# Cosformer attention and routed experts on one core: attention written out by hand as one pipeline, keys weighted in place of values, expert weights loaded later

## The chip, the core and the metric

The kernel runs on one core of one Trainium2 chip. A core has TensorE (PE; its weight loads are shown as PEld), VectorE (DVE), ScalarE (ACT), GpSimd (POOL) and SyncE (SP). Each works through its own queue of instructions in order; they wait for each other through semaphores. Sixteen DMA engines move data for all of them; here SP and POOL issue transfers. The metric is the device time of one execution in microseconds (us).

## What is computed

```python
def phi(x, c, s):
    r = np.maximum(x, 0.0)
    return np.concatenate([r * c, r * s], axis=-1)
q_p, k_p = phi(q, cos_w, sin_w), phi(k, cos_w, sin_w)      # 8 batches, 8 heads, 576 x 64
kv = np.einsum('bhsf,bhsd->bhfd', k_p, v)
z = np.sum(k_p, axis=2)
attn = einsum(q_p, kv) / (einsum(q_p, z) + 1e-06)
x = attn.transpose(0, 2, 1, 3).reshape(4608, 512)
...
e_idx = np.argmax(x @ w_gate, axis=1)                       # one of 8 experts for a row
gate_w, eom = probability of that expert, sigmoid(x @ w_output_gate)
ye = np.maximum(x[mask] @ w1[e], 0.0) @ w2[e]               # 512 -> 1024 -> 512
out[mask] = gate_w * eom * ye
```

`cos_w` and `sin_w` depend on the position in the sequence alone.

## The kernel before

**Attention.** A batch has 576 positions: four chunks of 128 (position 4p + c on partition p) and a tail of 64; the tails of two batches share a chunk. `stage_k` (L227 to 256) makes the product of keys and values of a batch. For each half of the heads ScalarE takes the relu of k (L235), VectorE multiplies each chunk of v by the cosine and by the sine into `vcs`, 64 + 1 columns each, the 1 being the weight itself for the sum `z` (L243, L245), and TensorE multiplies four heads, two at a time in the two column halves of its array, 64 weight columns (k) by 130 moving ones, into `kvp` (L252). In float32 one matmul leaves two records in the trace. `stage_g` (L257 to 282) copies `kvp` into `kvm`, transposes a copy of it (`kvtp`) and multiplies by the gate weights (`kvgp`, L276), so that `kvm` has 16 columns of logits more.

A unit is one chunk of queries of one batch, 36 in all (4 in an even batch, 5 in an odd one). `stage_q` (L284 to 335) sorts the heads (L292), transposes (L300), takes the relu on the way out (`qT`, L302), multiplies 16 records of 64 by 162 into `qo` (L311), joins the cosine and sine halves (`t` on ScalarE L322, `u` on VectorE L323), divides on GpSimd into a row `xr` of 512 float16 values (L333) and sums the logits into `glog` (L331). `u`, `t` and `qo` have two buffers each.

**Routing.** After each two batches `route` (L337 to 395) finds each row's expert, ranks it with small matmuls (L374, L376), and GpSimd scatters nine chunks of rows into the list `xs` in DRAM by indirect DMAs (L391). Then some 24 small instructions on VectorE (L429 to L468) turn the counts into 43 slots: the first row of each (`rows_i`) and its expert (`evs`).

**Experts.** For each slot SP loads 128 rows of `xs` (`fetch`, L488), TensorE transposes them (`xtsp`, L502), VectorE copies them (`xts`, L517), eight matmuls make `hp` (L522), ScalarE takes the relu (`hs`, L526). The transposes of `hs` (`htsp`, L511), their copy (`hts`, L514), eight matmuls into `yp` (L533), the scaling (`ysb`, L537) and the scatter to the output (L539) come one turn later. TensorE reads the slot's expert from `evs` into a register (L498) and addresses the weights with it.

**Order and transfers.** A scheduler orders the first part; in the last one the orders of PE and SP are as written. `load_w(e)` (L170 to 172) brings both matrices of an expert from float32 to float16 through POOL's queue, 1 MB each in SBUF. They have a place of their own, so nothing holds them back, and the calls of the first experts are issued at the start. k, v and q come through SP in halves of 512 KB. A scatter waits for the one before it, since both write `xs`.

## Time and profile before

| what | us |
|---|---|
| median of 2 runs (575.81 to 576.67) | 576.24 |
| profiled execution | 572.66 |
| its span | 570.9 |
| TensorE busy, share of the span | 352.1 (62%) |
| VectorE busy | 255.9 (45%) |
| ScalarE, GpSimd busy | 138.1, 140.6 |
| mean granted clock | 0.845 |

A row of the profile gives a line of the kernel, an engine, an operation with the tile that it writes and those that it reads, how often it ran, and times. "Idle before" is the time in which the engine had nothing running just ahead, with what ended that. The granted clock is TensorE's, as a share of 2.4 GHz. A busy TensorE is not TensorE at its peak.

### The profile page before, as it was taken

What the parts mean: (1) busy time and instruction counts of PE and PEld (TensorE: products, weight loads), DVE (VectorE), ACT (ScalarE), POOL (GpSimd) and SP (SyncE); (2) the same over time, 40 slices, a digit from 0 to 9 for tenths busy, and PEclk for the clock granted to TensorE, in tenths of its full rate; (3) what the DMA queues carried; (4) which work ended last, traced back from release to release, by engine and by line L of the source; (5) the groups of instructions that cost most, each with busy time, mean ns of one, the idle gap of its engine ahead of it and who ended that gap; (6) DMA issues with size and microseconds to landing.
All of it is one profiled execution on the core that took longest, in us unless ns stands there. A gap on an engine that the chain in (4) does not pass through costs nothing. (4 is left out here: it accounts for less than half of the span.)

```text
span 570.9 us, 8672 instructions
## 1 busy us (share of the span) xinstructions
PE 352.1 (62%) x2764; PEld 231.0 (40%) x2764; DVE 255.9 (45%) x851; ACT 138.1 (24%) x239; POOL 140.6 (25%) x189
## 2 busy tenths in 40 slices
PE   0020368443677578576683004888898888888883
PEld 0020257332555366455572002444444444444441
DVE  7011248424476578668665501333333333333331
ACT  0000025122152425253442000222222222222220
POOL 6100004112025232533345320211122222222221
PEclk9985659776597959789966555999999999999998
DMA  7999988999083708450310012112222222222200
GB/s 135 240 206 229 242 216 225 235 242 230 25 229 105 222 11 229 121 178 18 102 47 28 28 37 65 63 67 82 84 75 84 79 84 74 68 84 77 73 36 2
DMA packets 65755, 66.79 MB, mean 117 GB/s; under 512 B 18734, under 2 KB 58158, under 8 KB 65712
## 3 DMA queue, kind: packets, MB, share of 16 engines
q0 software_dynamic: 17712, 30.98, 23.0%
q1 hardware_dynamic: 48000, 35.26, 22.8%
q8 instruction: 25, 0.41, 0.3%
q14 instruction: 18, 0.15, 0.1%
HBM read 67.61 MB, written 17.22 MB: 149 GB/s over the span
## 5 line engine op out<-in xcount | busy, mean ns | idle before, releaser
L522 PE MATMUL hp<-w1t,xts 128*128 x344 | 83.2, 385 | 25.1 <-DVE xts L517 25.1
L526 ACT ACTIVATE hs<-hp 128x512 f16<-128x512 f32 x86 | 51.4, 597 | 191.5 <-PE hp L522 191.5
L252 PE MATMUL kvp<-vcs,k 128*64 128x130 f32 x512 | 48.7, 347 | 63.6 <-DVE vcs L245 57.5
L539 POOL DMA_INDIRECT out_dram<-ysb,sidx x43 | 42.1, 980 | 177.2 <-DVE ysb L537 163.7
L533 PE MATMUL yp<-w2t,hts 128*128 x344 | 81.3, 379 | 1.1 <-DVE hts L514 1.1
L311 PE MATMUL qo<-kvm,qT 64*128 64x162 f32 x512 | 56.0, 359 | 41.9 <-DVE u L323 32.1
L333 POOL TENSOR_TENSOR xr<-u,rc 128x512 f16<-128x512 f32 x36 | 39.6, 1104 | 128.0 <-DVE rc L327 127.5
L537 DVE TENSOR_SCALAR ysb<-yp,xg 128x512 f32<-128x512 f32 x43 | 32.3, 751 | 82.8 <-PE yp L533 82.8
L252 PEld LDWEIGHTS kvp<-vcs,k 128*64 128x64 f32 x512 | 39.6, 177 | 71.0 <-issue 57.1
L323 DVE SCALAR_TENSOR_TENSOR u<-qo,sinc,t 128x324 f32<-128x324 f32 x72 | 38.9, 551 | 64.0 <-ACT t L322 36.4
L311 PEld LDWEIGHTS qo<-kvm,qT 64*128 64x128 f32 x512 | 45.1, 221 | 51.2 <-DVE u L323 36.4
L391 POOL DMA_INDIRECT xs<-xr,di x36 | 37.7, 1047 | 89.9 <-DMA xs<-xr,di 63.3
L522 PEld LDWEIGHTS <-xts 128*128 128x128 f16 x344 | 33.7, 98 | 60.5 <-DVE xts L517 28.6
L322 ACT ACTIVATE t<-qo,cosc 128x324 f32<-128x324 f32 x72 | 37.7, 529 | 57.0 <-PE qo L311 42.2
L533 PEld LDWEIGHTS <-hts 128*128 128x128 f16 x344 | 33.6, 98 | 41.6 <-DVE hts L514 1.2
L243 DVE TENSOR_SCALAR vcs<-v,cosc 128x256 f32<-128x256 f32 x64 | 23.3, 365 | 46.1 <-DMA v<-in_v_dram 44.2
L504 DVE COPY_PREDICATED_SCALAR sidx<-valid,xg 128x1 int32 x43 | 9.3, 217 | 74.3 <-DMA xg<-xs 74.3
L502 PE MATMUL xtsp<-ident,xg 128*128 128x128 f16 x172 | 17.1, 224 | 34.1 <-DMA xg<-xs 34.1
L235 ACT ACTIVATE k<-k 128x1024 f32<-128x1024 f32 x16 | 16.9, 1056 | 87.4 <-DMA k<-in_k_dram 87.4
L502 PEld LDWEIGHTS <-xg 128*128 128x128 f16 x172 | 13.4, 100 | 44.4 <-DMA xg<-xs 34.1
L514 DVE COPY hts<-htsp 128x1024 f16<-128x1024 f16 x43 | 29.3, 681 | 0.4 <-PE htsp L511 0.4
L302 ACT ACTIVATE qT<-qtp 128x512 f32<-128x512 f32 x36 | 20.0, 595 | 34.6 <-PE qtp L300 34.6
(132 smaller groups left out, 363.3 us busy)
## 6 DMA issues: line engine op xcount, KB each, us to landing
w1t<-in_moe_w_dram POOLq DMA_DIRECT2D x8, 1024.0 KB, 28.4
w2t<-in_moe_w_dram POOLq DMA_DIRECT2D x8, 1024.0 KB, 28.7
k<-in_k_dram SPq DMA_DIRECT2D x16, 512.0 KB, 13.9
v<-in_v_dram SPq DMA_DIRECT2D x16, 512.0 KB, 9.9
q<-in_q_dram SPq DMA_DIRECT2D x16, 512.0 KB, 5.5
xg<-xs SPq DMA_DIRECT2D x43, 129.0 KB, 2.1
xs<-zt SPq DMA_DIRECT2D x9, 129.0 KB, 9.9
kt<-in_k_dram SPq DMA_DIRECT2D x8, 128.0 KB, 6.8
```

The costliest lines, as they stand in the source:

```text
L252: PE.matmul(kvp[64 * ab:64 * ab + 64, hf, 130 * pr:130 * pr + 130], lhs, w[p0:p1, h, :], start=(c == 0 and pr == 0), stop=(c == 4), skip_g ...
L311: PE.matmul(qo[:, 2 * ab + pr, 0:162], qT[r0:r0 + 64, qd, :], kvms[b][r0:r0 + 64, 2 * qd:2 * qd + 2, :], start=True, stop=True)
L322: ACT.activation(t[:], qo[:, :, 0:81], AF.Copy, scale=cosc[:, c:c + 1])
L323: DVE.scalar_tensor_tensor(u[:, 4 * hf:4 * hf + 4, :], qo[:, :, 81:162], sinc[:, c:c + 1], t[:], ALU.mult, ALU.add)
L333: GP.tensor_tensor(xrow[:, 0:DM].bitcast(F16).rearrange("p (h d) -> p h d", d=D), u[:, :, 0:64], rc[:].unsqueeze(2).to_broadcast([P, H, D] ...
L391: GP.indirect_dma_start(out=xs[:, :], out_offset=bass.IndirectOffsetOnAxis(ap=di[:, c:c + 1], axis=0), in_=xr[:], in_offset=None)
L502: PE.transpose(xts_ps[:, kc, :], xg[:, kc * 128:(kc + 1) * 128].bitcast(F16), ident16[:, :])
L522: PE.matmul(hp[:], xts[:, kc, :], w1t[:, kc, bass.ds(ev, 1), fh * 512:(fh + 1) * 512], start=(kc == 0), stop=(kc == 3))
L526: ACT.activation(hs[:, fh * 512:(fh + 1) * 512], hp[:], AF.Relu)
L533: PE.matmul(yp[:], hts[:, fc, :], w2t[:, fc, bass.ds(evp, 1), :], start=(fc == 0), stop=(fc == 7))
L537: DVE.tensor_scalar(ysb[:], yp[:], xgp[:, DM + 2:DM + 4].bitcast(F32), None, ALU.mult)
L539: GP.indirect_dma_start(out=out[:, :], out_offset=bass.IndirectOffsetOnAxis(ap=sidx[:, jj:jj + 1], axis=0), in_=ysb[:], in_offset=None, bo ...
```

## The change

**Keys weighted.** `k_prep` makes relu(k) times cosine on ScalarE and max(k times sine, 0) on VectorE into `kc`, 512 columns each, for a chunk of all eight heads. `k_mm` multiplies 16 times for a chunk, 64 weight columns (weighted k) by 65 moving ones: v as it came, with a column of ones behind it. For that column v is loaded into rows of 65 values, by head, in pieces of 256 bytes. `vcs` and its 40 small copies are gone. ScalarE takes the relu of q while it sorts the heads (`q_prep`); the copy after the transposes is a plain one.

**One order for all engines.** From the first load on the order of every engine is as written. A unit issues `q_mm`, the transposes of the next unit (`q_tr`), the planned chunks of the next batch's keys, its own output (`q_out`), the relu of the unit after next, and a piece of the route of the two batches before. The evacuation of the keys' product goes to VectorE and ScalarE by halves. Rows `xr` have 14 buffers in place of 10. Scatters to `xs`, and those to the output, are declared to touch distinct rows, so that one does not wait for another.

**Weights.** k, v and q are loaded into the place of the weights of experts 4 to 7, a batch ahead. Experts 0 to 3 are loaded at units 14, 19, 24 and 31, 4 and 5 after the last scatter, 6 and 7 after slots 2 and 4. Each load raises `wsem` by 32; a slot waits until it has 32 for each expert up to its own (`wns`), through a second register load.

**Experts.** The rows of slot j + 1 are transposed and copied before layer 1 of slot j; layer 2 of slot j - 1 follows it. Rows are fetched four slots ahead. `xtsp` has one buffer and `yp` two, where it was the other way.

Cut to its core:

```diff
-    vcs = []
-    for c in range(5):
-        t = constp.tile([P, 4, 130], F32, name=f"vcs{c}")
-        for h in range(4):
-            DVE.tensor_copy(t[:, h, 64:65], cosc[:, c:c + 1])
-            DVE.tensor_copy(t[:, h, 129:130], sinc[:, c:c + 1])
-        vcs.append(t)
...
+    EW = 4 * F + 8 * DM
+    wt = wpool.tile([P, E, EW], F16, name="wt")
+    w1v = wt[:, :, 0:4 * F].rearrange("p e (c f) -> p e c f", c=4)
+    w2v = wt[:, :, 4 * F:EW].rearrange("p e (c d) -> p e c d", c=8)
+    wsem = tc.alloc_semaphore("wsem")
...
+        for d in (GP.dma_start(w1v[:, e], moe_w1[e].rearrange("(c p) f -> p c f", p=128)),
+                  GP.dma_start(w2v[:, e],
+                               moe_w2[e].rearrange("(c p) d2 -> p c d2", p=128))):
+            d.then_inc(wsem, 16)
+            tc.add_to_no_dep_group("w", d.ins)
...
+    kbuf = [own(7, 4096 * i).rearrange("p (h c d) -> p h c d", h=H, d=D) for i in range(2)]
+    qbuf = [own(6, 4096 * i).rearrange("p (h c d) -> p h c d", h=H, d=D) for i in range(2)]
+    KW = H * NC4 * 65 * 2
+    v0 = wt[:, 4:6, :].rearrange("p e w -> p (e w)")
+    vbuf = [v0[:, KW * i:KW * i + KW].bitcast(F32).rearrange(
+        "p (h c d) -> p h c d", h=H, d=65) for i in range(2)]
+    for i in range(2):
+        GP.memset(vbuf[i][:, :, :, 64:65], 1.0)
+    vtl = constp.tile([P, H, 65], F32, name="vtl")
...
-        for e in range(E + 1):
-            SP.dma_start(xs[e * REG:e * REG + P, :], zt[:])
...
+        def load_v(b):
+            for h in range(H):
+                SP.dma_start(vbuf[b % 2][:, h, :, 0:D],
+                             v[b, h, 0:512, :].rearrange("(p c) d -> p c d", c=NC4))
...
+        def k_prep(b, c):
+            if c == 4 and b % 2 == 1:
+                return
+            nm = "kc" if c < 4 else "ktc"
+            kc = wk.tile([P, 2, H, D], F32, name=f"{nm}{b}_{c}", tag=nm,
+                         bufs=2 if c < 4 else 1)
+            src = kbuf[b % 2][:, :, c, :] if c < 4 else tails[b // 2, "k"][:]
+            ACT.activation(kc[:, 0], src, AF.Relu, scale=cosc[:, c:c + 1])
+            DVE.tensor_scalar(kc[:, 1], src, sinc[:, c:c + 1], 0.0, ALU.mult, ALU.max)
...
+            kc = kcs.pop((b, c)) if c < 4 else ktcs[b // 2]
+            p0, p1 = (0, P) if c < 4 else (lo, lo + 64)
             for hf in range(2):
-                kt, vt = kts[b, hf], vts[b, hf]
-                ACT.activation(kt[:], kt[:], AF.Relu)
-                ktl, vtl = tails[g, "k"], tails[g, "v"]
-                if par == 0 and hf == 0:
-                    ACT.activation(ktl[:], ktl[:], AF.Relu)
-                for c in range(5):
-                    w = vcs[c]
-                    p0, p1 = (0, P) if c < 4 else (lo, lo + 64)
-                    src = vt[:, :, c, :] if c < 4 else vtl[p0:p1, 4 * hf:4 * hf + 4, :]
-                    DVE.tensor_scalar(w[p0:p1, :, 0:64], src, cosc[p0:p1, c:c + 1],
-                                      None, ALU.mult)
-                    DVE.tensor_scalar(w[p0:p1, :, 65:129], src, sinc[p0:p1, c:c + 1],
-                                      None, ALU.mult)
-                    for pr in range(2):
+                for pr in range(2):
+                    for cs in range(2):
                         for ab in range(2):
-                            h = pr + 2 * ab
-                            lhs = (kt[:, h, c, :] if c < 4
-                                   else ktl[p0:p1, 4 * hf + h, :])
-                            PE.matmul(kvp[64 * ab:64 * ab + 64, hf,
-                                          130 * pr:130 * pr + 130],
-                                      lhs, w[p0:p1, h, :],
-                                      start=(c == 0 and pr == 0), stop=(c == 4),
-                                      skip_group_check=True)
-        def stage_g(b):
+                            h = 4 * hf + pr + 2 * ab
+                            rhs = (vbuf[b % 2][:, h, c, :] if c < 4
+                                   else vtl[p0:p1, h, :])
+                            o = 130 * pr + 65 * cs
+                            PE.matmul(kvp[64 * ab:64 * ab + 64, hf, o:o + 65],
+                                      kc[p0:p1, cs, h, :], rhs,
+                                      start=(c == 0 and pr == 0 and cs == 0),
+                                      stop=(c == 4), skip_group_check=True)
...
+            DVE.tensor_copy(kvm[:, 0:4, 0:65],
+                            kvp[:, 0, 0:260].rearrange("p (a w) -> p a w", w=65))
+            ACT.copy(kvm[:, 4:8, 0:65],
+                     kvp[:, 1, 0:260].rearrange("p (a w) -> p a w", w=65))
+            kvc = wk.tile([P, 8, 64], F32, name=f"kvc{b}", tag="kvc", bufs=1)
+            DVE.tensor_copy(kvc[:], kvm[:, :, 0:64])
...
+            qr = wk.tile([P, 2, 4, D], F32, name=f"qr{b}_{c}", tag="qr")
+            ACT.activation(qr[:], src.rearrange("p (a r) d -> p r a d", r=2), AF.Relu)
...
+                d = GP.indirect_dma_start(
+                tc.declare_no_dep(d.ins, group="sc", reason="distinct rows")
+                tc.add_to_no_dep_group("sc", d.ins)
+                if c % 3 == 2:
+                    yield
...
+        load_k(0)
+        load_v(0)
+        load_tails(0)
+        load_k(1)
+        load_v(1)
+        for e in range(E + 1):
+            SP.dma_start(xs[e * REG:e * REG + P, :], zt[:])
+        load_q(0)
...
+        plan_even = [[0, 1], [2, 3], [4]]
+        plan_odd = [[0], [1, 2], [3, 4]]
...
+        wload = {14: 0, 19: 1, 24: 2, 31: 3}
...
+            if c == 0:
+                if b + 1 < B:
+                    load_q(b + 1)
+                if b % 2 == 0:
+                    load_qtail(g)
+                if b + 2 < B:
+                    load_k(b + 2)
+                    load_v(b + 2)
+                if b % 2 == 1 and g + 1 < NG:
+                    load_tails(g + 1)
...
+            q_mm(b, c)
+            nxt = units[i + 1] if i + 1 < len(units) else None
+            if nxt is not None:
+                q_tr(*nxt)
...
+                        nc_ = rest[rest.index(cc) + 1:]
+                        if nc_:
+                            k_prep(b + 1, nc_[0])
+                        k_mm(b + 1, cc)
+                if c == len(plan) - 1:
+                    gst["kvc"] = g_evac(b + 1)
+                    gst["kvT"] = g_tr(b + 1, gst["kvc"])
+                elif c == len(plan):
+                    g_mm(b + 1, gst["kvT"])
+                    if b + 2 < B:
+                        k_prep(b + 2, 0)
+            xr = wk.tile([P, XW], U16, name=f"xr{b}_{c}", tag="xr", bufs=14)
+            xrows.append(xr)
+            q_out(b, c, glog, xr, len(xrows) - 1)
...
+            if i in wload:
+                load_w(wload[i])
...
+        load_w(4)
+        load_w(5)
...
+        DVE.tensor_scalar(wns[:], ej[:], 32.0, 32.0, ALU.mult, ALU.add)
...
+        def layer1(j):
+            ev = PE.value_load(evs[0:1, j:j + 1], min_val=0, max_val=7)
+            wv = PE.value_load(wns[0:1, j:j + 1], min_val=32, max_val=256)
+            PE.wait_ge(wsem, wv)
...
+        late = {2: 6, 4: 7}
...
+            if j + 4 < NSLOT:
+                fetch(j + 4)
+            if j + 1 < NSLOT:
+                x_tr(j + 1)
+            if j >= 1:
+                hts = h_tr(j - 1)
             if j < NSLOT:
+                layer1(j)
             if j >= 1:
+                layer2(j - 1, hts)
+            if j in late:
+                load_w(late[j])
         ctx2.close()
```

The order on TensorE in the first units of batch 0. `kvp` is the product of batch 1's keys, `qtp` the transposes of a unit, `qo` its products; x4 and x16 count like instructions. Before:

```order
L311 MATMUL qo_0_0_449<-kvm_340,qT_0_446 128x162
L252 MATMUL kvp_371<-vcs_142,k_0_359 64x130 x4
L252 MATMUL kvp_371<-vcs_151,k_0_359 64x130 x4
L252 MATMUL kvp_371<-vcs_160,kt_262 64x130 x4
L252 MATMUL kvp_371<-vcs_124,k_1_363 64x130 x4
L252 MATMUL kvp_371<-vcs_133,k_1_363 64x130 x4
L252 MATMUL kvp_371<-vcs_142,k_1_363 64x130 x4
L252 MATMUL kvp_371<-vcs_151,k_1_363 64x130 x4
L252 MATMUL kvp_371<-vcs_160,kt_262 64x130 x4
L311 MATMUL qo_0_0_449<-kvm_340,qT_0_446 128x162 x3
```

And now, from the first unit of batch 0 to the third:

```order
L340 MATMUL qo_0_0_389<-kvm_336,qT_0_357 128x162 x4
L340 MATMUL qo_0_1_397<-kvm_336,qT_0_357 128x162 x4
L322 MATMUL qtp_1_405<-ident,qr_1_350 128x128 x4
L272 MATMUL kvp_415<-wt,kc_0_369 64x65 x16
L272 MATMUL kvp_415<-wt,kc_1_412 64x65 x16
L340 MATMUL qo_1_0_462<-kvm_336,qT_1_410 128x162 x4
L340 MATMUL qo_1_1_470<-kvm_336,qT_1_410 128x162 x4
L322 MATMUL qtp_2_478<-ident,qr_2_459 128x128 x4
L272 MATMUL kvp_415<-wt,kc_2_432 64x65 x16
L272 MATMUL kvp_415<-wt,kc_3_485 64x65 x16
```

All chunks of the next batch stood inside the first unit; now they are shared out behind the units, 16 half as wide matmuls in place of 8 for a chunk.

The last scatters to `xs` on POOL, with what each waits for (DMASW3 is one of eight semaphores that POOL's transfers use in turn). Before:

```order
L390 COPY xr_4_2511<-meta_2582 128x2
L391 DMA xs<-xr_0_2210,di_2601 36992x516 [waits DMASW2_49,DVE_49,Pool_49]
L391 DMA xs<-xr_1_2245,di_2601 36992x516 [waits DMASW3_49,Pool_49]
L391 DMA xs<-xr_2_2280,di_2601 36992x516 [waits DMASW4_49,Pool_49]
L391 DMA xs<-xr_3_2315,di_2601 36992x516 [waits DMASW5_49,Pool_49]
```

And now, with the loads of experts 4 and 5 (L166 and L167) behind the last one:

```order
L427 COPY xr_0_2311<-meta_2768 128x2 [waits DVE_49]
L428 DMA xs<-xr_0_2311,di_2766 36992x516 [waits Pool_49]
L427 COPY xr_1_2391<-meta_2768 128x2
L428 DMA xs<-xr_1_2391,di_2766 36992x516 [waits DMASW4_49,Pool_49]
...
L427 COPY xr_4_2719<-meta_2768 128x2
L428 DMA xs<-xr_4_2719,di_2766 36992x516 [waits DMASW3_49,Pool_49]
L694 ISA [waits DMASW4_49]
L166 DMA wt<-in_moe_w_dram 128x4x1024 [waits DMAHW3_49,DMAHW4_49,DMAHW2_49,DMAHW5_49,DMAHW1_49,DMAHW6_49,DMAHW0_49,DMAHW7_49,DMASW4_49,PE_49]
```

Before, each waits for the semaphore of the one just ahead; now for that of eight transfers ahead, and the small copies stand between.

TensorE's queue in a slot of the experts, where the register load stands. Before, at the end of layer 2 of the slot ahead, and then the start of layer 1:

```order
L533 MATMUL yp_4048<-w2t,hts_4031 128x512
L498 TENSOR_LOAD evs
L498 ISA x2
L502 LDWEIGHTS xg_3939 [waits DMAHW2_49]
...
L511 MATMUL htsp_4088<-ident_69,hs_4035 128x128
L522 LDWEIGHTS xts_4099 [waits DVE_49]
```

And now:

```order
L607 LDWEIGHTS hs_3002 [waits Activation_49]
...
L607 MATMUL htsp_3048<-ident_69,hs_3002 128x128
L613 TENSOR_LOAD evs
L613 ISA x2
L614 TENSOR_LOAD wns
L614 ISA x2
L623 LDWEIGHTS xts_2969 [waits wsem]
```

One load stood behind layer 2 and ahead of the transposes of the rows; two stand now between the transposes of `hs` and layer 1, which waits for `wsem` and no longer for a copy on VectorE.

## Rows read from the trace of the kernel before

**Rows 1.** Timeline of SP's issues: start, us, queue, line, count.

```profile
3.57 5.66 SPq L193 DMA_DIRECT2D xs<-zt  x9
...
158.90 0.61 SPq L214 DMA_DIRECT2D vt<-in_v_dram  x1
```

**Rows 2.** Windows: stretch, us, busy PE, PEld, DVE, ACT, POOL, clock, DMA, GB/s.

```profile
180.00:313.00 133.00, 88.67 (x874) 68.95 (x871) 91.34 (x306) 48.36 (x88) 53.20 (x66) 0.84 0.37 109
313.00:350.50 37.50, 1.17 (x15) 0.91 (x15) 9.85 (x45) 0.47 (x2) 10.33 (x19) 0.50 0.12 39
350.50:562.60 212.10, 186.50 (x1200) 99.81 (x1199) 80.41 (x169) 51.36 (x86) 41.15 (x42) 0.99 0.21 71
```

**Rows 3.** Windows of line 331 alone, the sum of a unit's logits on VectorE.

```profile
180.00:313.00 133.00, 8.72 (x24) 0.84 0.37 109
```

**Rows 4.** Waits from 180 to 300: who waited for whom, us, times, longest.

```profile
POOL xs L391 <- DMA xs<-xr,di: 40.0, 15, 6.1
...
DVE u L323 <- POOL xr L333: 15.6, 6, 5.2
```

**Rows 5.** Timeline of one expert slot on TensorE and ScalarE.

```profile
433.60 1.89 PE L522 MATMUL hp<-w1t,xts 128*128 x8 [0.60 <-DVE xts L517]
...
438.48 1.89 PE L522 MATMUL hp<-w1t,xts 128*128 x8 [0.60 <-DVE xts L517]
...
440.21 1.89 PE L533 MATMUL yp<-w2t,hts 128*128 x8
...
440.41 0.60 ACT L526 ACTIVATE hs<-hp 128x512 f16<-128x512 f32 x1 [0.21 <-PE hp L522]
```

**Rows 6.** The page's DMA issues: KB each, median us to landing.

```profile
q<-in_q_dram SPq DMA_DIRECT2D x16, 512.0 KB, 5.5
```

**Rows 7.** Timeline of TensorE's weight loads in batches 5 and 6.

```profile
236.09 1.09 PEld L276 LDWEIGHTS kvgp<-wpr,kvT 128*128 128x128 f32 x8 [0.34 <-issue]
...
237.25 1.09 PEld L252 LDWEIGHTS kvp<-vcs,k 128*64 128x64 f32 x20
...
246.44 0.91 PEld L300 LDWEIGHTS qtp<-ident,qr 128*128 128x128 f32 x8 [0.34 <-issue]
...
247.85 1.13 PEld L311 LDWEIGHTS qo<-kvm,qT 64*128 64x128 f32 x16 [0.49 <-ACT qT L302]
```

**Rows 8.** Groups of instructions by line and form: count, busy us, mean ns.

```profile
L323 DVE SCALAR_TENSOR_TENSOR u<-qo,sinc,t 128x324 f32<-128x324 f32 x72 | 38.9, 551 | 64.0 <-ACT t L322 36.4 <-POOL xr L333 27.5
L322 ACT ACTIVATE t<-qo,cosc 128x324 f32<-128x324 f32 x72 | 37.7, 529 | 57.0 <-PE qo L311 42.2 <-PE qo L316 8.7 <-DVE rc L327 4.6
```

**Rows 9.** DMA queues in 295.5 to 303, 274.5 to 278, 30 to 60 (two rows).

```profile
q1 hardware_dynamic: 1152, 0.26, 15.9%
...
q1 hardware_dynamic: 489, 0.49, 46.2%
...
q0 software_dynamic: 3551, 4.62, 86.1%
q1 hardware_dynamic: 3550, 1.95, 30.7%
```

**Rows 10.** Timeline from the last logits to the first rows fetched.

```profile
312.57 0.37 DVE L331 TENSOR_REDUCE glog<-gl 128x16 f32<-128x128 f32 x1
...
317.43 1.00 POOL L391 DMA_INDIRECT xs<-xr,di  x1 [0.27 <-POOL xr L390]
...
344.44 0.97 POOL L391 DMA_INDIRECT xs<-xr,di  x1 [2.43 <-DMA xs<-xr,di]
347.22 22.81 SPq L488 DMA_DIRECT2D xg<-xs  x8
```

**Rows 11.** TensorE's sequencer in one slot: count, ns min/median/max, first and last start.

```profile
L498 PEldq TENSOR_LOAD <-evs x1: 303/303/303, 548.0 to 548.0; - x1
...
L498 PEldq SEQ_ASSERT  x1: 18/18/18, 548.6 to 548.6; - x1
...
L522 PEldq FUSED_REGOPS  x8: 51/55/55, 545.8 to 546.7; - x8
```

More of the change, by code (lines that the diff above doesn't have):

```diff
@@ new lines @@
+        plan_odd = [[0], [1, 2], [3, 4]]
+        k_prep(0, 0)
+        for c in range(5):
+            if c + 1 < 5:
+                k_prep(0, c + 1)
+            k_mm(0, c)
+        kvc = g_evac(0)
+        q_prep(0, 0)
+        kvT = g_tr(0, kvc)
+        q_prep(0, 1)
+        q_tr(0, 0)
+        g_mm(0, kvT)
+        k_prep(1, 0)
+        pending = []
+        gst = {}
+        wload = {14: 0, 19: 1, 24: 2, 31: 3}
+        for i, (b, c) in enumerate(units):
+            g = b // 2
+            if c == 0:
+                if b + 1 < B:
[7 more added lines that the diff above has]
+                    load_tails(g + 1)
+            if b % 2 == 0 and c == 0:
@@ new lines, in layer2 @@
+        def layer2(j, hts):
+            ev = evr.pop(j)
+            xg = xgs.pop(j)
+            yp = ps_y.tile([P, DM], F32, name=f"yp{j}", tag="yp")
+            for fc in range(8):
+                mm = PE.matmul(yp[:], hts[:, fc, :],
+                               wt[:, bass.ds(ev, 1),
+                                  4 * F + fc * DM:4 * F + fc * DM + DM],
+                               start=(fc == 0), stop=(fc == 7))
+                tc.declare_no_dep(mm.ins, group="w", reason="waits on wsem")
+            ysb = fsb.tile([P, DM], F32, name=f"ysb{j}", tag="ysb", bufs=5)
+            DVE.tensor_scalar(ysb[:], yp[:], xg[:, DM + 2:DM + 4].bitcast(F32),
+                              None, ALU.mult)
+            d = GP.indirect_dma_start(
+                out=out[:, :],
+                out_offset=bass.IndirectOffsetOnAxis(ap=sidx[:, j:j + 1], axis=0),
+                in_=ysb[:], in_offset=None,
+                bounds_check=N - 1, oob_is_err=False)
+            tc.declare_no_dep(d.ins, group="so", reason="distinct rows")
+            tc.add_to_no_dep_group("so", d.ins)
```

343 lines of the change are left out of this document (162 added, 181 removed).

## The prediction

> **What bounds the kernel now.** I read first the windows view, cut at the stage borders. The profiled execution has a span of 570.9 us and took 572.66, so 1.8 us lie around the span. The span itself shows no single full engine (TensorE 62%, VectorE 45%). From 180 on the expert weights are loaded, and the attention runs undisturbed to 313: 133 us in which TensorE is busy 67% and VectorE 69%, at a granted clock of 0.84 and a DMA share of 0.37 [rows 2]. A count of the last VectorE instruction of a unit (a unit is one chunk of 128 query rows of one batch) gives 24 units there [rows 3], so 5.54 us for one, and no engine is full. The waits of that stretch name the reason: the scatter of finished rows to `xs` waits for the scatter before it (40 us), and VectorE waits for GpSimd to free `u` (15.6 us) [rows 4]. From 313 to 350.5 TensorE is nearly idle [rows 2], and there nine such scatters stand one behind the other. Then 43 expert slots take 212.1 us at a clock of 0.99 [rows 2], 4.88 us from one first-layer start to the next, 0.60 of it a wait for the copy of `xts` [rows 5]. After the last matmul 8.3 us remain.
>
> **The change part by part.** I add up the changed kernel's own stages, not differences.
>
> *Start.* `zt` and all early weights stood ahead of the first loads of k and v; now k and v come first. Ahead of q(0) SP issues 4 gate loads, 4 halves of k, 16 heads of v, 4 tails and 9 times `zt`. A load of 512 pieces costs 0.61 of SP, nine `zt` 5.66 [rows 1]; halves of k and q I take at 0.4, as estimates. That is 0.8 + 2.6 + 1.6 + 20 x 0.61 + 5.7 + 0.8, so q(0) is issued by 23.7 and lands 5.5 later [rows 6], at 29.2. Two 0.6 us passes of ScalarE and four transposes later, at **31.5**, the first unit can begin. The keys of batch 0 are done under this (VectorE has cosc and sinc at about 12, since the 40 small copies into `vcs` are gone). Unhidden they would cost some 10 us.
>
> *What a unit costs TensorE.* Sixteen records of L311 make 1.13 us, and four transposes half of 0.91 [rows 7], so 1.59 in each unit. The key product is the open price. Before, one chunk of keys was 8 matmuls of 64 weight columns by 130 moving ones; now it is 16 of 64 by 65. A matmul leaves two records; 20 records took 1.09 at a clock of 1.00, so 54 ns each [rows 7]. If a record follows the moving columns, 65 make it 27, and a chunk of 32 records costs 0.87 as before. If it follows the weights, it stays 54, and a chunk costs 1.74. The nearest row is `kvgp`: only 64 moving columns, yet 8 records took 1.09, 136 ns each, with 128 weight columns [rows 7]. Its time goes with the weights, so I take **1.74**; 0.87 stays as the lower bound. The Trainium skill (TensorE: Matmul & The Clock Gate, LDWEIGHTS) speaks against this edit as well: loading weights takes time by their columns, about 53 ns for 64 (an estimate from its formula), whatever is streamed behind them. No run here shows a 64 by 65 matmul. By counting moving columns the whole would come to about 399, by the rule to 430.
>
> *Units.* The plan gives the 4 units of an even batch 2, 2, 1, 0 chunks of the next batch, and the 5 of an odd one 1, 2, 2, 0, 0. So 3.33 with one chunk, 5.07 with two. In the unit with the last chunk TensorE then waits for two evacuations that follow each other (0.42 each, worked out from 0.53 for the 324 columns of `t` [rows 8]), a copy of about 0.55 and three hand-offs of 0.2, then transposes again: 2.4 more. A unit without a chunk is bound by its chain: half a product 0.56, hand-off 0.2, twice 0.53 for `t` [rows 8], 0.60 for `qT`, with hand-offs about 2.9. Even: 5.07 + 5.07 + 5.73 + 2.9 = 18.8; odd: 3.33 + 5.07 + 7.47 + 2.9 + 2.9 = 21.7. Three such pairs and a last one without keys behind it (18.8 + 14.5) make 154.8. TensorE's own share is 3 x 32.6 + 23.5 = 121; at a clock of 0.9, a little above the 0.84 of [rows 2] as it is busier, it grows by 13. With 2 for the weight loads it is **170**, or 4.7 a unit.
>
> What this hides: weighting k instead of v leaves VectorE one 512-column pass in place of four of 256 per chunk, and the relu of q moves to ScalarE. VectorE then has two `u` of 0.55 [rows 8], about 1.15 of small work and 0.5 to 1.1 for k, ScalarE two `t`, `qT`, `qr` and one or two k passes, 2.3 to 3.5. Both lie under TensorE's 5.07 or just fill 2.9; without that cover ScalarE's 0.6 a chunk would cost 24 us. GpSimd has 1.1 for `xr` and three scatters of 1.2 in some units; it no longer waits for the previous scatter. v is now in 256-byte pieces, because a row in SBUF carries a one behind 64 values. 1152 packets, nearly all of this size, took 15.9% of 16 engines for 7.5 us, 16.6 ns each, and 489 of 1 KB 53 ns each [rows 9]. A batch of k, v, q and tails is then 6.8 + 4.2 + 1.6 = 12.6 us of the engines, against 19 to 22 us per batch: hidden.
>
> The last unit ends at 31.5 + 170 = **201.5**.
>
> *Gap.* Before, 4.5 us go by from the last logits (312.9) to the first scatter, then eight more start, one each 3.4; the last at 344.44, and SP fetches at 347.22 [rows 10]. The scatters are now declared independent: 1.0 of GpSimd [rows 10] plus a copy of 0.2. So 3.5 + 9 x 1.2 + 1.8 for the last landing, and from fetch to matmul 3.3 as before, to which I add 4 because two experts' weights are queued behind the last scatter and share the engines: **24**, against 37.5.
>
> *Experts.* With `xts` made a slot ahead the 0.60 goes: 4.88 - 0.60 = 4.28. But layer 1 now stands behind two register loads between the transposes of `hs` and its first weights. One load with its register work runs from 548.0 to 548.6 [rows 11]. `hs` is ready 0.80 after the first layer ends [rows 5]; half of the transposes (0.3), two loads (1.26) and one address step (0.13 each [rows 11]) follow, with hand-offs 2.6 to 2.7, while the array has work for 4.28 less the 1.73 of a layer, 2.55. The sum over the sequencer, 16 x 0.13 + 1.26 + 12 transposes at some 0.08, is 4.3 too. I take 4.40 (4.28 if all hides, 4.88 if the wait only changes its name): 43 x 4.40 + 2.3 for the ends, as before, = **191.5**. Weight waits cost nothing if the weights are there. Routing the inputs by the reference gives 3, 4, 5, 0, 8, 5, 4, 10 tiles for experts 0 to 7, and four empty slots that count as expert 7. Expert 4 is wanted at slot 12, 53 us into this stage; its load is issued some 8 us before the stage, and one expert is 11.7 us of all engines (86.1% of 30 us for 4.62 MB [rows 9]). Without that cover 20 to 30 us would stand here.
>
> *Sum.* 201.5 + 24 + 191.5 + 8.3 + 1.8 = 427, against 572.7 of the same execution. The median of the runs, 576.24, lies 0.6% higher, so I predict **430**.
>
> **Rivals.**
> - *Key matmuls shrink with their moving columns.* 0.87 a chunk. ScalarE then bounds units with two chunks (3.5): 14.8 + 18.1 a pair, some 131 in all. But eight batches of 12.6, four experts of 11.7 and `zt` are 151 us of transfers, so the last unit isn't over before about 170. Time 399. Against it speaks `kvgp`.
> - *Hand-offs keep the old pace.* If in-order queues idle as the scheduler's did, 5.54 a unit: 36 x 5.54 = 199, time 460. For it: no engine was full before. Against: the two largest waits there are removed.
> - *Weight loads starve k, v and q.* While weights ran, SP's queue moved 1.95 MB in 30 us [rows 9], and a batch needs 3.5 MB. Expert loads 0 to 2 fall into units that still load. If each delays a batch by 10 to 20, the time is 460 to 490.
> - *Late experts hold the slots.* If experts 4 to 7 land after they are wanted, 20 more: 450.
> - *TensorE falls to the lower clock.* If the two register loads leave gaps in each slot that take the granted clock from 2.4 to 1.2 GHz, a slot costs 8.6 and all 43 give 614, slower than before. It decides from 34 slots on (146 / 4.28). Against: the 0.60 gap in every slot left the clock at 0.99 [rows 2, 5].
>
> **How the numbers follow.** My own sum 0.50 (its range 412 to 446), shrinking key matmuls 0.12, old pace 0.20, starved loads 0.12, late experts 0.03, lower clock 0.03. The likeliest is 430. The range 398 to 475 leaves out half of the first rival, a third of the starved loads and the clock, 0.13. Only the clock ends above the old time; a mixture of the middle ones could end within 2%, which is about what a measurement can tell from no change. So faster 0.95, same 0.02, slower 0.03.
>
> **What would show it.** First unit's L340 near 31; 36 units in 170; records of L272 at 54 ns at full clock (27: the first rival); no wait of xs on xs; 24 from the last logits to L623; slots 4.3 to 4.5 apart, without a wait for `wsem` after slot 0. Wrong would be units over 5.3, waits for k or v in the middle, or slots over 4.7.

## The result and the profile after

The changed kernel takes **437.3 us** (median of two runs, 435.65 and 438.95) against 576.24: a ratio of 0.759, with a 95% interval of 0.746 to 0.771. The forecast was 430, its own range 412 to 446. The total is right; the stages it was added up from are less so, and their errors have both signs. The profiled execution took 435.65 with a span of 433.8:

| stage | forecast | measured |
|---|---|---|
| first unit begins | 31.5 | 38.4 |
| 36 units | 170 | 173.6 (38.4 to 212.0) |
| last logits to first L623 | 24 | 32.1 (to 244.1) |
| 43 slots and their ends | 191.5 | 181.1 (to 425.2) |
| tail, around the span | 8.3 + 1.8 | 8.6 + 1.85 |
| sum | 427 | 435.6 |

The windows of the changed kernel at the same borders (stretch, us, busy PE, PEld, DVE, ACT, POOL, clock, DMA, GB/s):

```profile
0.00:38.40 38.40, 10.76 (x184) 9.44 (x185) 9.64 (x72) 7.89 (x12) 2.63 (x25) 0.82 0.99 220
38.40:212.00 173.60, 127.24 (x2070) 107.16 (x2071) 108.11 (x328) 100.70 (x191) 79.32 (x98) 0.89 0.81 187
212.00:244.00 32.00, 1.76 (x18) 1.21 (x18) 11.26 (x50) 0.47 (x2) 14.75 (x23) 0.50 0.61 134
244.00:425.00 181.00, 178.45 (x1192) 96.40 (x1193) 75.91 (x167) 51.29 (x86) 45.12 (x46) 0.99 0.47 120
```

Against [rows 2], a part of the old units, TensorE is busy 73% of the units, not 67%, and in the slots it has no pause left (178.45 of 181). The DMA share in the units went from 0.37 to 0.81: the loads that before stood ahead of everything now run beside the units.

The units are not of one pace. The windows of line 366 alone (a unit's logits, as in [rows 3]), cut after the 10th, 19th and 28th unit:

```profile
38.40:80.90 42.50, 3.72 (x10) 0.96 0.83 204
80.90:122.00 41.10, 3.34 (x9) 0.92 0.83 215
122.00:177.40 55.40, 3.34 (x9) 0.82 0.99 215
177.40:212.10 34.70, 2.96 (x8) 0.91 0.47 88
```

From the end of unit 0 (44.7) to that of unit 9 (80.6) nine units, a pair of batches, take 35.9, 4.0 each, where the forecast had 40.5. The next nine take 41.1, the nine behind them 55.4. Had all gone at the pace of the first pair, the units would have lasted 148.9: 21 less than forecast, and 25 less than they took. Of the 25, 5 stand in the second pair, at the first one's DMA share of 0.83, and 19.5 in the third, where the share is 0.99. The 25 is rather too much: the first pair has no scatters of a pair ahead to do, and in seven of the runs below it took 36.9 to 37.2.

### The profile page after: what moved, and what is told of

The parts are those of the page before. It is cut to its first block, busy times and chain, and to the rows that moved or that the text cites. A ratio compares the mean times of both kernels' runs of the same rounds, so it can differ in the third digit from the quotient of the medians.

```text
span 433.8 us, 10053 instructions
## 1 busy us (share of the span) xinstructions
PE 319.4 (74%) x3468; PEld 214.5 (49%) x3468; DVE 205.7 (47%) x616; ACT 160.4 (37%) x291; POOL 142.8 (33%) x192
## 4 chain that ended last, share of the span: by engine, by line
issue 31%; DMA 18%; PE 17%; POOL 13%; DVE 8%; SPq 7%; ACT 3%; POOLq 1%; another core or an unknown queue 0%; DVEq 0%; ACTq 0%
DMA xs<-xr,di 12%; POOL out_dram L643 9%; PE qo L340 6%; PE kvp L272 6%; SPq L218 4%; DMA wt<-in_v_dram 4%; PE qtp L322 3%; POOL xs L428 3%; DVE u L352 2%; DMA wt<-in_q_dram 2%; DMA vtl<-in_v_dram 1%; ACT t L351 1%; SPq L447 1%; DVE kc L251 1%; PE kvtp L294 1%
## 5 line engine op out<-in xcount | busy, mean ns | idle before, releaser
L623 PE MATMUL hp<-wt,xts 128*128 x344 | 82.5, 383 | 2.4 <-DVE sidx L600 1.2
L635 PE MATMUL yp<-wt,hts 128*128 x344 | 81.3, 379 | 1.1 <-DVE hts L609 1.1
L272 PE MATMUL kvp<-wt,kc 128*64 128x65 f32 x1024 | 41.4, 240 | 22.5 <-ACT kc L250 13.8
L340 PE MATMUL qo<-kvm,qT 64*128 64x162 f32 x512 | 48.3, 331 | 8.7 <-ACT qT L324 2.7
L272 PEld LDWEIGHTS kvp<-wt,kc 128*64 128x64 f32 x1024 | 36.9, 152 | 27.9 <-issue 14.6
L623 PEld LDWEIGHTS <-xts 128*128 128x128 f16 x344 | 32.6, 99 | 34.2 <-issue 3.0
L351 ACT ACTIVATE t<-qo,cosc 128x324 f32<-128x324 f32 x72 | 36.9, 529 | 30.7 <-PE qo L340 25.1
L340 PEld LDWEIGHTS qo<-kvm,qT 64*128 64x128 f32 x512 | 40.3, 203 | 12.9 <-ACT qT L324 6.2
L322 PE MATMUL qtp<-ident,qr 128*128 128x128 f32 x144 | 25.4, 303 | 13.1 <-ACT qr L315 13.1
L598 DVE COPY xts<-xtsp 128x512 f16<-128x512 f16 x43 | 17.8, 414 | 20.7 <-PE xtsp L595 19.7
L607 PE MATMUL htsp<-ident,hs 128*128 128x128 f16 x344 | 26.4, 219 | 0.2 <-ACT hs L628 0.2
L322 PEld LDWEIGHTS qtp<-ident,qr 128*128 128x128 f32 x144 | 16.3, 149 | 20.0 <-ACT qr L315 14.9
```

What stands on the lines that cost most here:

```text
L272: PE.matmul(kvp[64 * ab:64 * ab + 64, hf, o:o + 65], kc[p0:p1, cs, h, :], rhs, start=(c == 0 and pr == 0 and cs == 0), stop=(c == 4), skip ...
L322: PE.transpose(tp[:, i, :], qrf[:, 128 * i:128 * i + 128], ident[:])
L340: PE.matmul(qo[:, 2 * ab + pr, 0:162], lhs, kvms[b][r0:r0 + 64, 2 * qd:2 * qd + 2, :], start=True, stop=True)
L351: ACT.activation(t[:], qo[:, :, 0:81], AF.Copy, scale=cosc[:, c:c + 1])
L623: mm = PE.matmul(hp[:], xts[:, kc, :], wt[:, bass.ds(ev, 1), kc * F + fh * 512:kc * F + fh * 512 + 512], start=(kc == 0), stop=(kc == 3))
L635: mm = PE.matmul(yp[:], hts[:, fc, :], wt[:, bass.ds(ev, 1), 4 * F + fc * DM:4 * F + fc * DM + DM], start=(fc == 0), stop=(fc == 7))
```

## The experiments

All times stand beside 437.3, and beside 572 to 576 of the kernel before, run again with each of them. A time with an interval is the median of four executions, which differ by 3 to 5 us; one without is a single execution. By the total, k130, w_early, sc_chain, load3 and all3 lie clear of 437.3; the others do not, and of these the stages of the profile are read.

**1. The price of a key matmul (two runs).** The forecast took 54 ns a record, 1.74 us a chunk. Here only the moving columns change:

```diff
-PE.matmul(kvp[..., hf, o:o + 65], kc[..., h, :], rhs)
+PE.matmul(kvp[..., hf, 130*pr:130*pr + 130], kc[..., h, :], v of heads h2, h2 + 1)   # k130
+PE.matmul(kvp[..., hf, o + 32:o + 65], kc[..., h, :], rhs[:, 32:65])                 # k33, chunks 1 to 4
```

> Each key matmul streams 130 columns (two heads' values) behind the same 64 weight columns, in place of 65; the number of matmuls stays. What it changes of the computation: each head's keys are also multiplied with a neighbouring head's values, and two products fall on the same columns. In the changed kernel 32 records of L272 take 1.15 us at full clock, 36 ns each, where the prediction took 54. Theory A, a record is paid partly by the moving columns (54 at 130 before, 36 at 65 now): 32 records take about 1.73 again, and an undisturbed pair of batches, 36 to 40 us now, grows by 10 chunks of 0.58, so by up to 5.8. Theory B, it is paid by the weights alone and something else made them cheaper: 1.15 stays, and so does the time.

> Each key matmul but those of a batch's first chunk streams 33 columns (the upper half of the values and the ones) instead of 65; the lower 32 values get the first chunk's sums alone, so the attention's values are wrong. The chunk of 32 records took 3.78 / 2 = 1.89 us with 130 columns and 1.15 with 65 at full clock, 59 and 36 ns a record. Theory A, a line through the two: 13 ns and 0.354 for each column, so 33 columns give 25 ns a record and 0.79 a chunk; units with two chunks last 0.7 less, the total falls by 5 to 8, to 429 to 433. Theory B, with fewer columns the 64 weight columns set the price, and 36 is near that floor (kvgp, 64 weight columns and 32 moving ones, shows 41 in the changed kernel): 1.0 to 1.3 a chunk, total 434 to 440.

TensorE's timeline at full clock, of the changed kernel (matmuls, then their weight loads), of k130 and of k33 (start, us, line, shape, records):

```profile
61.79 1.15 PE L272 MATMUL kvp<-wt,kc 128*64 128x65 f32 x32
...
61.79 1.01 PEld L272 LDWEIGHTS kvp<-wt,kc 128*64 128x64 f32 x32 [0.17 <-issue]
```

```profile
47.39 3.78 PE L273 MATMUL kvp<-wt,kc 128*64 128x130 f32 x64
```

```profile
61.83 1.13 PE L273 MATMUL kvp<-wt,kc 128*64 128x33 f32 x32
```

With 130 columns 32 records take 1.89, with 65 they take 1.15, with 33 still 1.13. So the price is the larger of two: up to 65 moving columns it is a floor, 36 ns a record; above it grows with the columns. k130 took 452.7, 15.4 more, its first pair 42.7 instead of 35.9 (6.8 more; up to 5.8 was expected). k33 took 441.9, no less. Theory A of k130 holds between 65 and 130, theory B of k33 below.

The starts of the single records say what the floor is. They come in pairs, 5 to 7 ns apart: the two heads of a pair stand in the two column halves of the array. From one pair to the next go 58 to 59 ns with 65 columns and with 33, and 111 with 130. So from start to start a record costs 29 ns, and the 36 holds the end of the last one as well. The `kvgp` of the kernel before has 128 weight columns by 64 moving ones; here it is at full clock:

```profile
97.78 0.97 PEld L276 LDWEIGHTS kvgp<-wpr,kvT 128*128 128x128 f32 x8 [0.17 <-issue]
```

Its records fill both halves and start one by one, 111 to 112 ns apart (160 behind the first). With as many moving columns, twice the weight columns thus cost nearly twice the floor, so the floor goes with the weights and is no fixed price of a record. A chunk costs TensorE 16 pairs of 58.5, 0.94 us, where the kernel before paid 8 pairs of 110, 0.88: the edit made the matmuls hardly dearer. The Trainium skill (TensorE: Matmul & The Clock Gate, Step-by-step: what each phase is for) says that the next weights load while the current matmul streams, at a time that goes by weight columns; these rows agree with both.

**2. Where the experts' loads stand (two runs).**

```diff
+for e in range(4): load_w(e)          # w_early: ahead of load_k(0)
-wload = {14: 0, 19: 1, 24: 2, 31: 3}
+wload = {}                            # w_early
+wload = {27: 0, 29: 1, 31: 2, 33: 3}  # w_170
```

> The weights of experts 0 to 3 are issued ahead of all loads, as in the kernel before; nothing else is undone. Theory A, the order of the loads was a large part of the gain: four experts of 11.7 us of all 16 DMA engines stand in the way of the first k, v and q, so the first unit starts near 75 instead of 38.4; the units then take 155 instead of 173.5, since no expert comes between them; total 455 to 465. Theory B, the engines had room and only the hand-written pipeline counts: the first unit starts by 50 and the total stays under 440.

> The weights of experts 0 to 3 are issued at units 27, 29, 31 and 33, after the last load of k, v and q, instead of at units 14, 19, 24 and 31. Theory A, the 19 us that two units lost between 139 and 166 were taken by the experts' loads, which filled the DMA engines while v, k and the tails of batch 6 were waited for: those waits go, the units take about 155 instead of 173.5; the four experts take 47 us from about 160 on, the first is there before slot 0 and the fourth long before slot 12; some us come back as slower scatters and fetches; total 417 to 424. Theory B, the waits come from SyncE's queue, which issues the loads in order and late, whatever the experts do: the units stay over 168 and the total over 432.

w_early took 465.05: theory A, though its units took 163.7 and not 155. Its first unit starts at 80.6; in the changed kernel the order of the loads is worth 28 of the 139 us gained. w_170 took 433.1 (ratio to before 0.753, interval 0.748 to 0.758) and its units 172.0: these are theory B's numbers. But the third pair moved as theory A said. In the changed kernel, the waits from 100 to 172 name what is late (who waited for whom, us, times, longest), and SyncE's own row shows eight heads of v taking 18.5 us to issue:

```profile
PE kvp L272 <- DMA wt<-in_v_dram: 7.6, 2, 4.9
...
PE kvp L272 <- DMA vtl<-in_v_dram: 6.2, 1, 6.2
DVE ktc L251 <- DMA kt<-in_k_dram: 5.0, 1, 5.0
```

```profile
112.20 18.47 SPq L218 DMA_DIRECT2D wt<-in_v_dram  x8
```

In w_170 the same windows of line 366 read:

```profile
83.50:128.00 44.50, 3.33 (x9) 0.92 0.76 196
128.00:172.00 44.00, 3.34 (x9) 0.92 0.53 145
172.00:211.30 39.30, 2.96 (x8) 0.83 1.05 184
```

The third pair fell from 55.4 to 44.0 (45.7 in w_early): the experts' loads were what its data waited for. But 44 is still 8 above the first pair, the second pair rose from 41.1 to 44.5, and the last eight units, with the four experts in them and a DMA share of 1.05 instead of 0.47, rose from 34.7 to 39.3. So the gain was mostly given back. Why the last units grew stays open; it isn't VectorE's wait for GpSimd, which is as long in the changed kernel from 177 to 212 as in w_170 from 190 to 250:

```profile
DVE u L352 <- POOL xr L360: 7.8, 3, 4.1
```

```profile
DVE u L352 <- POOL xr L360: 8.0, 2, 4.9
```

**3. v once (one run).** Is it the amount of data as such?

```diff
 if b + 2 < B:
     load_k(b + 2)
-    load_v(b + 2)
```

> v is loaded for batches 0 and 1 alone (and all tails); batches 2 to 7 use the values of 0 and 1 again, so their results are not the reference's. Everything else is as in the changed kernel, the experts' loads too. It takes 6 of 8 batches' 4096 pieces of 256 bytes from the DMA engines, some 25 us of all of them by 16.6 ns a piece, and 48 issues from SyncE. Theory A, the arrival of data sets the pace between 95 and 170, whoever is late: the pairs of batches that took 40 and 52 us take 34 to 36, as the pair without late data in the run with early weights, and the units end 15 to 20 us earlier, near 193, total 417 to 424. Theory B, the long units come from the engines' hand-offs and the change of batches: the units end after 205, total over 430.

It took 433.2. The windows of line 366, third pair, and the share of DMA there:

```profile
123.00:173.80 50.80, 3.33 (x9) 0.76 1.04 224
```

Theory A falls in this form: with three quarters of v gone, the third pair still takes 50.8 with full DMA engines; the experts' loads are in the same place, and k, q and the tails remain. It fell by 4.6, where taking the experts' loads away made it 11.4 less: their place counts for more than the bytes of v.

**4. v in pieces of 1 KB (one run).**

```diff
-SP.dma_start(vbuf[b % 2][:, h, :, 0:D], ...)      # 256-byte pieces
+SP.dma_start(vbuf[b % 2][:, h] as 260 columns, 0:256, ...)
```

> v is loaded in pieces of 1 KB instead of 256 bytes, over the column of ones, so the normaliser and the values of the attention are wrong; the number of bytes, matmuls and passes stays. By the rows of before, 16.6 ns for a piece of 256 bytes and about 50 for 1 KB, v costs the 16 engines 34 us in all and would cost 26. Theory A, the DMA engines stand close to the path in the units (share 0.82 to 0.98): the units end 5 to 10 us earlier, and SyncE's issue of a head of v falls from 0.9 to 1.3 us towards 0.6. Theory B, only the experts' loads make the units wait: no more than 2 us less.

It took 433.7, the units end 2.9 earlier, and the first starts at 35.0. SyncE's first two rows of eight heads, of the changed kernel and of this one:

```profile
4.79 6.15 SPq L218 DMA_DIRECT2D wt<-in_v_dram  x8
...
15.09 7.93 SPq L218 DMA_DIRECT2D wt<-in_v_dram  x8
```

```profile
4.79 4.78 SPq L219 DMA_DIRECT2D wt<-in_v_dram  x8
...
13.59 5.38 SPq L219 DMA_DIRECT2D wt<-in_v_dram  x8
```

A head's issue falls from 0.77 and 0.99 to 0.60 and 0.67, as theory A said; the 5 to 10 us at the end of the units don't come. What the column of ones costs is shown for the start alone: 35.0 against 38.4 to 39.7 in the runs that start alike. The units themselves last as long (174.1), and the total is within what two executions differ by.

**5. The start (one run).**

```diff
+load_q(0)
 load_k(1)
 load_v(1)
-for e in range(E + 1): SP.dma_start(xs[...], zt[:])   # now behind the loads of batch 1's first unit
-load_q(0)
```

> q of batch 0 is loaded ahead of k and v of batch 1, and the nine zt writes are issued behind the loads at batch 1's first unit. Theory A, the first unit waits only for that q, which stands behind 25 us of SyncE's issuing: the first unit starts near 27 instead of 38.4, some 4 us come back while k and v of batch 1 are waited for, total 428 to 431. Theory B, the DMA engines are the bound from the start (share 0.96 up to 31.5): the same bytes have to come before the units can go on, what is gained at the first unit is lost by the ninth, total 434 to 438.

It took 432.6 (0.750, 0.744 to 0.755). TensorE's row of its first unit, and the windows of line 366 behind it:

```profile
24.81 1.37 PE L340 MATMUL qo<-kvm,qT 64*128 64x162 f32 x16 [0.48 <-DVE kvm L307]
```

```profile
33.00:74.00 41.00, 3.35 (x9) 0.92 0.99 240
...
115.50:174.00 58.50, 3.35 (x9) 0.82 1.00 217
```

The first unit starts 13.6 earlier, and 10.5 of that is gone at the end of the units (208.9): the first pair takes 41.0 instead of 35.9, the third 58.5 instead of 55.4, both with a DMA share of 0.99 or more. Both theories were half right; it is nearer to B.

**6. Scatters in a chain again (one run).**

```diff
-tc.declare_no_dep(d.ins, group="sc", reason="distinct rows")
-tc.add_to_no_dep_group("sc", d.ins)
```

> The scatters into xs are no longer declared independent, as in the kernel before; nothing else is undone. Theory A, each then waits for the one ahead to land, 3.4 apart as in the kernel before: nine of them add 9 x 1.95 = 17.6 us between the last logits and the first expert matmul, and in a pair of batches GpSimd has 9 x (1.1 + 3.4) = 40.5 us, as much as a pair lasts (36 to 40), so another 5 to 15 in the units: total 460 to 470. Theory B, the landing is mostly hidden by the copy and the row product between two scatters: total 440 to 446.

It took 502.7, 65 more than the changed kernel and far over theory A's 470. Its waits from 38 to 312:

```profile
DVE u L352 <- POOL xr L360: 81.6, 10, 16.5
POOL xs L428 <- DMA xs<-xr,di: 81.4, 25, 11.8
```

A wait for the scatter ahead is 3.3 in the mean and up to 11.8, not always 1.95 more. The two longest, 9.3 until 171.4 and 11.8 until 259.3, are those behind an expert's load issued in the same GpSimd queue, at 149.9 and 243.0. VectorE waits as long for `u`. The units end at 266.9, and the stretch behind them takes 44. So in this kernel the independence of the scatters is worth more than twice the order of the loads. That the two go together, late experts being affordable only because no scatter waits for another, is likely by this, but no run has the chain with early experts.

**7. The stretch behind the last logits (one run).**

```diff
-di = small("di", [P, GC], I32)                      # one buffer
+di = wk.tile([P, GC], I32, tag="di", bufs=2)
 for c in range(GC):
-    GP.tensor_copy(xr_c[:, DM:DM + 4], meta[:, c, :])
+    GP.tensor_copy(xr_{c+1}[:, DM:DM + 4], meta[:, c + 1, :])
     GP.indirect_dma_start(...)
```

> Two buffers for di in place of one, and the copy of a row's two extra columns made one scatter ahead, so that no scatter waits for its own copy. In the changed kernel the last routing waits 2.7 us at L419 until an earlier scatter has read di, and nine scatters then start 1.45 apart: 0.97 for itself, 0.19 for the copy, 0.28 of wait for it. Theory A, both stand on the path between the last logits and the first expert matmul: the 2.7 goes and the scatters start 1.17 apart, so 5.2 us less there, total about 432. Theory B, something else ends that stretch (the fetch behind the weights of experts 4 and 5): it stays at 32 and the total at 435 to 439.

The changed kernel's timeline there:

```profile
211.67 0.36 DVE L366 TENSOR_REDUCE glog<-gl 128x16 f32<-128x128 f32 x1
...
217.79 0.17 DVE L419 CAST di<-df 128x9 int32<-128x9 f32 x1 [2.69 <-DMA xs<-xr,di]
...
218.64 1.01 POOL L428 DMA_INDIRECT xs<-xr,di  x1 [0.28 <-POOL xr L427]
...
230.57 0.97 POOL L428 DMA_INDIRECT xs<-xr,di  x1 [0.28 <-POOL xr L427]
...
234.08 24.30 SPq L588 DMA_DIRECT2D xg<-xs  x8
...
240.75 0.61 PE L595 MATMUL xtsp<-ident,xg 128*128 128x128 f16 x4 [26.70 <-DMA xg<-xs]
```

and that of the run:

```profile
222.52 1.01 POOL L435 DMA_INDIRECT xs<-xr,di  x1 [0.16 <-POOL xr L427]
...
233.47 0.97 POOL L435 DMA_INDIRECT xs<-xr,di  x1 [0.19 <-POOL dum L434]
```

The last logits end there at 218.5, the first L623 (there L630) is at 246.5: 28.0 instead of 32.1. The wait for `di` is gone, and scatters start 1.37 apart, not 1.17 (a wait of 0.16 stays). Theory A holds for the stretch. The total of 436.5 (0.758, 0.754 to 0.762) doesn't show it: in the profiled execution (438.4) the units took 5 us longer, most of it in the second pair, and whether that comes of the change isn't shown. Fetches issued at 236.1 reach TensorE 7.1 later, with two experts in the queues.

**8. A third register load (one run).**

```diff
 ev = PE.value_load(evs[0:1, j:j + 1], min_val=0, max_val=7)
 wv = PE.value_load(wns[0:1, j:j + 1], min_val=32, max_val=256)
+PE.value_load(evs[0:1, j:j + 1], min_val=0, max_val=7)
```

> A third register load on TensorE in each expert slot, its value not used. In the changed kernel a slot is 4.12 us, the array without a pause, and the two loads run on the sequencer while the array still has matmuls of layer 2 to do; the first address step of layer 1 comes about 0.15 us ahead of its matmul. Theory A, the two loads just fit: a third, 0.70, makes a slot 0.55 longer, 4.67, and the total 24 us longer, near 461. Theory B, the queue in front of the array hides a third too: a slot stays at 4.12 to 4.2.

It took 470.3, 33 more: slots of 4.77 in the median instead of 4.12. That is theory A, a little dearer than it said (0.65 a slot, not 0.55). First layers of two slots, of the changed kernel and of this one:

```profile
266.11 1.89 PE L623 MATMUL hp<-wt,xts 128*128 x8
...
270.24 1.89 PE L623 MATMUL hp<-wt,xts 128*128 x8
```

```profile
266.38 1.89 PE L624 MATMUL hp<-wt,xts 128*128 x8 [0.44 <-issue]
...
271.19 1.89 PE L624 MATMUL hp<-wt,xts 128*128 x8 [0.53 <-issue]
```

TensorE's sequencer in one slot of the changed kernel (count, ns, first and last start):

```profile
L613 PEldq TENSOR_LOAD <-evs x1: 301/301/301, 272.9 to 272.9; - x1
...
L614 PEldq TENSOR_LOAD <-wns x1: 301/301/301, 273.6 to 273.6; - x1
```

```profile
L614 PEldq SEQ_ASSERT  x2: 18/18/18, 270.0 to 274.3; - x2
```

Both loads lie between 272.9 and 274.3, while the array still does layer 2 of the slot ahead and the transposes. The next first layer begins at 274.44, 4.20 behind the one before instead of 4.12: here the array had to wait 0.08. So the loads hide, with nothing to spare, and a third puts 0.65 into every slot.

**9. Versions meant to be faster (two runs).** Both take the start of 5, the two changes of 7, two scatters a unit instead of three, and later experts:

```diff
+wload = {24: 0, 26: 1, 28: 2}; late = {0: 3, 1: 4, 2: 5, 3: 6, 4: 7}      # all1
+wload = {24: 0, 26: 1, 28: 2, 30: 3}; load_w(4) behind the last scatter
+late = {1: 5, 3: 6, 5: 7}; 20 buffers for xr; zt at batch 2               # all3
```

> A version meant to be faster than both: q of batch 0 first and zt behind batch 1's loads; experts 0 to 2 at units 24, 26 and 28; experts 3 to 7 one a slot from slot 0 on, so that none stands between the last scatter and the first fetch; two di buffers, the copy one scatter ahead, two scatters a unit instead of three. Theory A, the data arrives early enough once the experts stand behind it, and the parts add: first unit near 25, the units end near 190, then 24 to 25 us to the first expert matmul, slots of 4.12: total 400 to 408. Theory B, the sum of all transfers up to the last batch still sets the end of the units, near 205, and only the stretch behind them gets shorter: 420 to 428.

> The former combined version with its two new waits taken away: experts 0 to 3 at units 24, 26, 28 and 30 and 20 buffers for xr in place of 14, so that no row product waits for scatters that stand behind the experts in GpSimd's queue (7.2 us there); expert 4 behind the last scatter, 5 to 7 at slots 1, 3 and 5 instead of five in a row, so that the rows out are not held up behind them (24 us in slots 7 to 10 there); zt one batch later. Theory A, those two waits were all that was lost: the units end near 187, 26 us later the slots begin, 4.12 each to the end: 402 to 408. Theory B, whatever stands in GpSimd's queue comes back at the next place where its transfers are waited for: 415 or more.

all1 took 430.1 (0.747, 0.742 to 0.751): its units end at 193.3 and the slots begin at 218.6, 25 us sooner than in the changed kernel, and then slots 7 to 10 take 9.6, 11.3, 11.2 and 5.4 (from one `ysb` to the next). GpSimd's rows of it name the queue twice, in the units and in the slots:

```profile
186.26 1.04 POOL L361 TENSOR_TENSOR xr<-u,rc 128x512 f16<-128x512 f32 x1 [7.16 <-DMA xs<-xr,di]
```

```profile
251.39 0.90 POOL L167 DMA_DIRECT2D wt<-in_moe_w_dram  x1 [7.61 <-DMA out_dram<-ysb,sidx]
```

Rows of `xr` and of `ysb` come free only when their scatters have landed, behind the experts' loads, of which five stand in a row in the slots. all3, with more buffers and the experts spread, took **411.8** (0.716, 0.710 to 0.721), 6% below the changed kernel:

```profile
24.00:182.20 158.20, 125.45 (x2070) 105.39 (x2071) 105.74 (x329) 101.18 (x192) 74.48 (x95) 0.93 0.92 217
182.20:214.50 32.30, 1.76 (x18) 1.25 (x18) 14.30 (x49) 0.47 (x2) 17.95 (x28) 0.50 0.82 177
214.50:400.00 185.50, 180.40 (x1196) 96.80 (x1195) 75.97 (x167) 51.28 (x86) 46.91 (x48) 0.99 0.46 117
```

The units take 158 instead of 173.6 and begin 14 earlier. The stretch behind them is still 32, where all1 had 25.3: with expert 4 behind the last scatter it takes 10.3 from the first fetch to the first layer, in all1, with none there, 5.2. And one slot of 7.2 has a wait of 5.4 for a row out. Neither theory's total was met (theory A 402 to 408, theory B 415 or more): those two waits were most of what was lost, and some of it came back.

## Why the prediction was right, step by step

- *Start, 6.9 too early.* The step that failed is the issue price: 0.61 for a load of 512 pieces was that of a single load [rows 1]; with 16 heads in a row and a DMA share of 0.99 a head took 0.77 and 0.99. So q(0) was issued from 27.7, 4.0 late, and used at 35.15, 7.5 later instead of 5.5 [rows 6]. Experiment 5 shows that a right start would have changed the end by only 3 us.
- *Key matmuls, the term that was mis-sized.* 1.74 a chunk was forecast, from weight loads of 54 ns; the same kind of row now shows 1.01 (32 ns), and the matmuls' row 1.15. The step that failed is the reading of `kvgp` [rows 7] as the price of a key record. Its 136 ns hold some time at the lower clock (0.88 in the mean from 236.09 to 237.25; at full clock it is 121), and it has twice the weight columns, so its records stand alone where two of the keys run side by side. And 54 was the price of 130 moving columns. The first rival (27 ns, 0.87 a chunk) was nearer than the sum; what kept it from being met is the floor of the weights. In the units the error was worth less than 35 x 0.59 = 20.7. The sum also held 13 for a clock of 0.9, and the first pair ran at 1.00: without the 13, 157 stand against the undisturbed 148.9, 8 less. By k130, where 0.74 more a chunk made the units 16.4 longer, 0.59 is worth some 13 (an estimate). A wider bound on each side would have been the honest reading of the two rows; the range had them, the sum did not.
- *Starved loads, a rival at 0.12, came true in part.* The third pair took 19.5 more than the first, and its waits name v, its tail and k, the rival's mechanism. By w_170 and w_early some 10 to 11 of that go with the two experts' loads, so the size was the rival's lower end, once and not for each batch. The other 8 or 9, and the 5 of the second pair, stand in no term of the sum. Together they cancelled what the sum had too much; that the total was right is in this part luck. One of the forecast's own signs of being wrong, waits for k or v in the middle, did come.
- *Old pace of hand-offs.* Fell: 4.0 a unit where nothing is late and 4.8 over all, against 5.54 [rows 3].
- *No wait of a scatter on a scatter.* Right, and worth 65 us with the late experts (experiment 6); the forecast had priced only its 37.5 to 24 in the stretch and "they no longer wait" in the units.
- *The stretch of 24.* Too short by 8.1, and its own terms add up to 23.4. What it lacked: the wait for `di` (2.7), scatters 1.45 instead of 1.2 apart (2.3 in all, as each waits 0.28 for its own copy), and 10.0 from the first fetch to L623 instead of 7.3.
- *Slots, 4.40.* Measured 4.12, below the bound of 4.28. The array's own work is 16 x 0.216 + 12 x 0.055 = 4.1, and nothing else is left in a slot. The bound was not one: the named wait of 0.60 is counted from the modelled end of the last transpose, while by the starts the array stood 0.76 in each old slot (4.88 - 4.12), and all of it went. The two register loads were priced as if they ran after the transposes of `hs`; the sequencer runs them ahead of the array (experiment 8).
- *Clock and late experts.* Both fell: a clock of 0.99 in the slots, and L623 waits for weights once, 1.2 us at slot 1.

**What stays open.** With the experts out of the units (w_early, w_170) pairs with scatters still take 41 to 46 instead of 36 to 37, at a DMA share of 0.5 to 0.8. The profile puts pauses of 2 to 3 us there to no releaser that it knows. Two scatters a unit and the copy ahead, together with later experts, brought the third pair to 37.7 in all3; which of them did it wasn't separated. The order of the loads (28) and the independent scatters (65) were each undone alone, so they need not add up, and no run undoes the weighting of the keys or the hand-written order: what these two are worth by themselves isn't shown.

## What to carry to other kernels

When loads are moved off the front of a kernel, cost them again where they land: a load that shares a queue with small transfers delays each wait and each buffer behind it, so spread them, and give the buffers in that queue the depth of the longest load. A price per instruction is read only from rows with the same weight columns, moving columns and granted clock, and with the same neighbour beside it in the array; where two of them differ, both ends belong in the sum. And a total that comes out right is checked stage by stage before its reasons are believed.

## What the runs showed of the hardware

A float32 matmul leaves two records. With 64 weight columns, two records in the two column halves of the array cost 58.5 ns together from start to start, whether 33 or 65 columns move, and 111 at 130; with 128 weight columns and 64 moving ones a record stands alone and costs 112 (changed kernel, k33, k130, kernel before, all at full clock). From one register load on TensorE to the next its sequencer takes 0.70; two of them hide in a slot of 4.12, a third adds 0.65 (load3). With the scatters in a chain, the longest wait for a scatter behind an expert's load in GpSimd's queue was 11.8 (sc_chain), and an expert's load waited 7.6 for a scatter behind other experts (all1). The Trainium skill (DMA: Bandwidth & Descriptors, Two DMAs through the same engine are not ordered) says that within one queue of one engine transfers start in order; the 7.6 and 11.8 fit that. Issuing a head of v in 512 pieces costs SyncE 0.77 us at the start and 2.3 (18.47 for eight) from 112 on, where GpSimd's queue takes 71% of the engines' time; in 128 pieces of 1 KB it costs 0.60 at the start.
